# Chunked delta-rule attention with a Mish layer: T~ of 64 tokens merged on TensorE, W = T~K had ahead, attention in fixed bundles

## The chip, the core and the metric

One core of a Trainium2 chip runs the kernel; the time is device time in microseconds from the start of the program to its end. The engines named below work side by side, each through its own list of instructions in order: PE (TensorE, matrix products), DVE (VectorE), ACT (ScalarE), POOL (GpSimd), and SP (SyncE), which issues the loads and stores. Results of TensorE land in PSUM, everything else lies in SBUF, whose 128 rows are the partitions.

## The reference

Four batches of eight heads, 768 tokens, 48 dimensions a head. Each head keeps a state of 48 x 48 that is read and corrected token by token; the outputs of all heads of a token make a row of 384, and go through a layer of width 2048 with Mish.

```python
k_n = k / (norm(k) + 1e-6)
for t in range(S):
    y[:, :, t] = einsum('bhd,bhde->bhe', q[:, :, t], state)
    v_old = einsum('bhde,bhd->bhe', state, k_n[:, :, t])
    state = state + beta_t * einsum('bhd,bhe->bhde', k_n[:, :, t], v_t - v_old)
...
x = y.transpose(0, 2, 1, 3).reshape(B * S, H * D)
h = x @ w_in
sp = where(h > 20, h, log1p(exp(minimum(h, 20))))
out = (h * tanh(sp)) @ w_out
```

## The kernel before

The tokens are cut into 12 chunks of 64. Attention of a chunk is done in matrix form: with c the length of a key plus 1e-6, b' = beta / c^2, V' = c V and L the strictly lower part of K K^T, a chunk solves (I + L b') Z = V' - K S, takes Z~ = b' Z, adds K^T Z~ to the state S, and its output is Y = Q S + lower(Q K^T) Z~. The matrix T~ = b' (I + L b')^-1 turns the solve into a product. The 32 heads are 16 pairs; a pair shares instructions.

**Early part, for two chunks at once (`early`).** VectorE transposes K to `kt`, TensorE makes the Gram blocks `pg`, VectorE masks them to `d` and transposes them to `gt`, so that one block of 32 x 32 lies in each partition. After the norms (`ss`, `nb`, the product at L273) a forward substitution of 30 steps, each one product (`pr`, L290) and one addition (`gt`, L295), gives the inverse; L297 multiplies by b', and L301 transposes to `tt`. For the first group blocks are 16 wide and `merge` completes them. For the second group the steps j = 1 to 17 run on GpSimd and the rest on VectorE; for later groups all run on VectorE.

**Attention of a chunk (`step`), a quarter of the pairs (one batch) at a time.** T~ is had for blocks of 32 tokens only, so a chunk is solved in two halves. `s1`: transpose of Q, Q's and the state's product with K in one go (`gq`, 112 columns), V' less K S. `s2`: Z~ of tokens 0 to 31 (`za`). `s3`: what those do to tokens 32 to 63 (`pr`, L413). `s4`: Z~ of the latter (`zb`). `s5`: Y (`py`, L431) and the new state (`ps`, L437). A tile `xx` for each batch holds, in 64 rows for tokens, Z~, lower(Q K^T) and K and, in the other 64 rows, S, Q^T and rows of the identity. One product with all 128 rows therefore gives Y, and one gives the new state, the identity carrying the old one over.

**The layer (`moe`).** For each chunk there are eight units. `g1`: 18 products to `h`. Then a chain over `e` on ScalarE and VectorE (L509 to L514), a split to `g` (L522, L525). `g2`: 12 products to `acc`. Two tiles of `h` exist, so the third `g1` waits until the first `e` is done. Products are in float32r with values split in a high and a low part. When a chunk's eight units are through, ScalarE copies `acc` to `o` (L551) and the rows are stored.

**The weights** come as float64, in 28 parts (`ri`, `ro`), and are converted on the chip: four instructions of VectorE for most parts (L180, L182, L187, L189 on `mi`, `mo`), two of ScalarE, one of GpSimd (L199).

**The order.** Every piece of work is put on a plan with a time in units of a chunk's layer (`put`); the pieces are written out in the order of these times, a scheduler orders each engine's list for the first part of the plan, and VectorE's instructions that pass `queue` keep their order. Pieces of attention of the next chunk are spread between the units of the layer.

Of the kernel before, what the change touches and what calls it, by code (L numbers as in the profile page):

```python
# [8 lines left out]
F32 = mybir.dt.float32  # L9
# [7 lines left out]
# float32 values whose bits are 0x38000000 and 0x47EFFFFF: the high words of float64s of  # L17
# float32's least and largest exponent
# [15 lines left out]
def kernel(  # L34
# [22 lines left out]
    nc = tc.nc  # L57

    TN = dict(c=[(-2.89,0),(-2.88,0),(-2.8,0),(-2,3),(-1.951,3+3),(-1,11),(0.5,28)],a1=-0.05,a2=0.15,s2a=0.85,s2b=1.1,kp=0,kl=0.15,pp=[0,0.1,0.3,0.5,0.6,0.8],ke=0.1,d0=["k0","k1",1,"b"],d1=["q","v",2,"x",3,"k2",0,"k3",6],p1=-1.4,lo=150,sg=4,wm=14,wpg=8,e1a=-0.7,e1b=0.4,jt=5,wt=46,qk=99,qg=1,qs=1,k2a=-0.95,k2b=-0.6,wmg=18,wz=[4,4,4,4],wgq=2,ma=-0.98,mb=-0.98+0.1,pg=3,fg=1,ps=(1,),e2=1.1,mt=(-1.95,-1.95+0.05),qt=[(-1.95,-1.95+0.1),(-1.6,-1.6+0.1)],st=[(-1.9,-1.9+0.05),(-1.75,-1.75+0.05),(-1.55,-1.55+0.05),(-1.2,-1.2+0.2)],j0=0,j1=18)
# [11 lines left out]
    PB = NP // B  # L71
# [5 lines left out]
    kk = k.rearrange("b (p hh) t d -> hh t (b p) d", hh=2)  # L77
    qq = q.rearrange("b (p hh) t d -> hh t (b p) d", hh=2)
    vv = v.rearrange("b (p hh) t d -> hh t (b p) d", hh=2)
    bt = beta.rearrange("b (p hh) (g t2 c i) -> hh c t2 (b p) g i", hh=2, t2=2, c=2, i=32)  # L80
# [20 lines left out]
    # lmask[p, f] = f >= p % 32 ; amask[(hh,c,j), i] = i > 32c + j  # L101
# [11 lines left out]
    # per batch and head, tokens' rows: Z~ | Aqk^T | K  # L113
    # and rows of d:                    S  | Q^T   | rows of the identity
    W = C + 2 * D
    xx = [cp.tile([P, PB, 2, W], F32, name=f"xx{i}") for i in range(B)]
    for t in xx:
        nc.gpsimd.memset(t[:, :, :, 0:D], 0.0)
        for hh in range(2):
            r = slice(64 - 64 * hh, 128 - 64 * hh)  # L120
            nc.vector.tensor_copy(t[r, :, hh, D + C:], bcast_mid(ident[r, r.start:r.start + D], PB))

    # parts of the weights, each first as float64 and then, in the same place, as high and low parts
# [5 lines left out]
    def load(dst, src):  # L129
        """Loads of the start are issued in this order."""  # L130
        m = nc.sync.dma_start(out=dst, in_=src)  # L131
        if loaded and len(loaded) < TN.get('lo', 150):
            order(m, loaded[-1])
        loaded.append(m)

    def load_src(dst, src, n):
        for hh in range(2):
            for ch in range(2):
                w = 32 if ch == 0 else D - 32
                for tb in range(2):  # L140
                    t0 = C * n + 32 * tb
                    r0 = 64 * (1 - hh) + 32 * ch
                    load(dst[r0:r0 + 32, :, tb, :w], src[hh, t0:t0 + 32, :, 32 * ch:32 * ch + w])

# [13 lines left out]
    def queue(ins, on=True):  # L158
        """VectorE issues what passes here in this order, and the rest where it fits."""
# [11 lines left out]
    def convert(kind, i):  # L171
# [5 lines left out]
        # magnitudes outside float32's exponents go to 0 or the largest  # L177
        # and 2^-80 of the rest has bits that, moved up by 3, are float32's of -|w|
# [5 lines left out]
        # the sign comes by VectorE or, while VectorE is what holds the start up, by the others  # L184
# [18 lines left out]
    kts, tts, nes, ats, vts, dts, tus, yms = {}, {}, {}, {}, {}, {}, {}, {}  # L203

    def early(g):
        dt = ap.tile([P, 2, NP, 32], F32, tag="d", name=f"d{g}", bufs=2)
        split = g < FG
        dts[g] = dt
        for t2 in range(2):
# [5 lines left out]
            kt = kts[n] = ap.tile([P, NP, 2, 32], F32, tag="kt", name=f"kt{n}", bufs=4)  # L215
# [8 lines left out]
            at = ats[n] = ap.tile([P, NP, 32], F32, tag="at", name=f"at{n}", bufs=4)  # L224
            for h8 in range(2):
                ps = pa.tile([P, 8, C], F32, tag="at", name=f"pg{n}_{h8}")
                for p8 in range(8):
                    p = 8 * h8 + p8
                    # rows c = 0: K0 K0^T, K0 K1^T; rows c = 1: K1 K1^T twice
                    for c in range(2):  # L230
                        for hh in range(2):
                            r = slice(64 - 64 * hh, 128 - 64 * hh)
                            r0 = 64 * hh + 32 * c
                            mv = kt[r, p] if c == 0 else kt[r, p, 1:2, :].broadcast_to([64, 2, 32])
# [4 lines left out]
                nc.vector.tensor_tensor(out=dt[:, t2, pr, :], in0=ps[:, :, 0:32],  # L239
                                        in1=bcast_mid(lmask, 8), op=ALU.mult)  # L240
                nc.scalar.copy(out=at[:, pr, :], in_=ps[:, :, 32:])
# [25 lines left out]
        # N[i, j] = -G[i, j] b'_j ; X = (I - N)^-1 in place  # L267
# [32 lines left out]
        tt = tts[g] = ap.tile([P, 2, NP, 32], F32, tag="tt", name=f"tt{g}")  # L300
        queue(nc.vector.transpose(tt.rearrange("p a b i -> p i (a b)"), gt), qg)  # L301
        if split:
# [4 lines left out]
            nc.gpsimd.memset(ym[:, :32, 16:], 0.0)  # L307
        yield

    def merge(n):  # L310
        """T~'s rows 16.. and columns ..15 of each block of 32: -T~22 G21 T~11."""
        g, t2 = n // 2, n % 2
        dt, tt, tu, ym = dts[g], tts[g], tus[g], yms[g][:, NP * t2:NP * t2 + NP]
        pm = {}
# [12 lines left out]
        for h8 in range(2):  # L327
# [6 lines left out]
            if g == 0:  # L334
                keep_warm(TN.get('wmg', 1), m)
            queue(nc.vector.tensor_tensor(out=tt[:, t2, pr, 16:32], in0=tt[:, t2, pr, 16:32], in1=ps, op=ALU.add),
                  n < QS)
            yield

# [5 lines left out]
    def load_v(n):  # L345
        for h8 in range(2):
            vt = vts[n, h8] = ap.tile([P, 8, D], F32, tag="vt", name=f"vt{n}_{h8}", bufs=3)
# [3 lines left out]
    def load_k(n, b):  # L351
        for hh in range(2):
            load(xx[b][64 * hh:64 * hh + 64, :, hh, D + C:], kk[hh, C * n:C * n + C, PB * b:PB * b + PB])

    def step(n, y):
        g, t2 = n // 2, n % 2
        kt, at, ne = kts[n], ats[n], nes[g]

        def scale_v(b):
            vt = vts[n, b // 2][:, PB * (b % 2):PB * (b % 2) + PB, :]  # L360
            nc.gpsimd.tensor_tensor(out=vt, in0=vt,  # L361
                                    in1=bcast_in(ne[:, 16 * t2 + PB * b:16 * t2 + PB * b + PB], D), op=ALU.mult)

        def s1(b, half=None):
            pr = slice(PB * b, PB * b + PB)
            p8 = slice(PB * (b % 2), PB * (b % 2) + PB)
            vt, x = vts[n, b // 2], xx[b]
            if n:
                scale_v(b)
            for hh in range(2 if half != 1 else 0):  # L370
                r = slice(64 - 64 * hh, 128 - 64 * hh)
                queue(nc.vector.transpose(x[r, :, hh, D:D + C], qsrc[r, pr].rearrange("p a b c -> p a (b c)")), n == 0)  # L372
            if half == 0:
                return
            # S is 0 in the first chunk
            d = D if n else 0
            ps = pa.tile([P, PB, C + d], F32, tag="at", name=f"gq{n}_{b}")
            for p in range(PB):
                for hh in range(2):
                    r = slice(64 - 64 * hh, 128 - 64 * hh)  # L380
                    m = nc.tensor.matmul(ps[64 * hh:64 * hh + 64, p, :], kt[r, PB * b + p], x[r, p, hh, D - d:D + C],  # L381
                                         start=True, stop=True)
            if n == 0:
                keep_warm(TN.get('wgq', 1), m)
            if n:
                nc.vector.tensor_tensor(out=vt[:, p8, :], in0=vt[:, p8, :], in1=ps[:, :, 0:D], op=ALU.subtract)
            for hh in range(2):
# [351 lines left out]
```

## Time and profile before

| | |
|---|---|
| time, median of 3 runs (lowest to highest) | 741.7 us (740.0 to 743.1) |
| span of the profiled execution | 745.6 us |
| instructions in it | 22768 |
| TensorE busy, share of the span | 92% |
| VectorE, ScalarE, GpSimd busy | 72%, 63%, 17% |
| granted clock of TensorE, mean | 0.95 |
| weights converted until | 172.7 us |
| first and last output copies | 175.2 us, 734.3 us |

The busy shares are means over stages of unlike kind: the first 200 us have the loads and conversions of the weights, the first chunks' attention and the first units of the layer, the rest is a steady alternation of attention and layer. A row of the chain of waits gives the start, the length and the instructions of one engine on the path that ended last; a row of the grouped view gives a line, its engine and operation, the tile written and the tile read, shapes and count, then the busy time, the mean of one in ns, and the idle time ahead of them. For products in float32 the trace shows two records for each instruction.

### The profile page before, as it was taken

What the parts mean: (1) busy time and instruction counts of PE and PEld (TensorE: products, weight loads), DVE (VectorE), ACT (ScalarE), POOL (GpSimd) and SP (SyncE); (2) the same over time, 40 slices, a digit from 0 to 9 for tenths busy, and PEclk for the clock granted to TensorE, in tenths of its full rate; (3) what the DMA queues carried; (4) which work ended last, traced back from release to release, by engine and by line L of the source; (5) the groups of instructions that cost most, each with busy time, mean ns of one, the idle gap of its engine ahead of it and who ended that gap; (6) DMA issues with size and microseconds to landing.
All of it is one profiled execution on the core that took longest, in us unless ns stands there. A gap on an engine that the chain in (4) does not pass through costs nothing.

```text
span 745.6 us, 22768 instructions
## 1 busy us (share of the span) xinstructions
PE 682.3 (92%) x9656; PEld 602.3 (81%) x9674; DVE 534.3 (72%) x1152; ACT 468.9 (63%) x1005; POOL 127.4 (17%) x171
## 2 busy tenths in 40 slices
PE   5659699878799989999999999999999999999993
PEld 3236588768788878998898998998988989989993
DVE  5796999997747997659995579975499964454351
ACT  2233667755485666776776767767767767767681
POOL 3431336894221221000000000000000000000000
PEclk9756999789899999999999999999999999999998
DMA  5762910253213032122222221130130120000000
GB/s 87 185 181 40 380 32 7 30 84 60 25 32 59 8 54 48 21 44 50 37 34 41 40 38 34 24 51 15 24 59 14 33 49 18 18 23 1 17 7 21
DMA packets 160981, 37.75 MB, mean 51 GB/s; under 512 B 154224, under 2 KB 157296, under 8 KB 160880
## 3 DMA queue, kind: packets, MB, share of 16 engines
q1 hardware_dynamic: 160880, 36.30, 24.0%
q8 instruction: 76, 1.25, 0.7%
q14 instruction: 25, 0.20, 0.1%
HBM read 31.56 MB, written 4.72 MB: 49 GB/s over the span
## 4 chain that ended last, share of the span: by engine, by line
PE 67%; DVE 20%; SPq 4%; issue 3%; ACT 2%; DMA 2%; POOL 1%; DVEq 0%; POOLq 0%; ACTq 0%
PE h L505 24%; PE acc L535 22%; PE gq L381 4%; SPq L131 3%; PE py L431 3%; PE pg L235 2%; PE za L398 2%; DVE pr L290 2%; PE zb L398 2%; PE pr L413 2%; DVE gt L295 2%; PE warm L570 2%; PE ps L437 2%; DVE e L514 1%; DVE xx L389 1%
## 5 line engine op out<-in xcount | busy, mean ns | idle before, releaser
L505 PE MATMUL h<-x,wi 128*128 128x256 f32 x1728 | 238.3, 291 | 13.5 <-DVE e L514 12.1
L505 PEld LDWEIGHTS h<-x,wi 128*128 128x128 f32 x1728 | 218.4, 192 | 23.8 <-DVE e L514 12.5
L535 PE MATMUL acc<-wo,g 128*128 128x384 f32 x1152 | 233.4, 350 | 2.3 <-ACT g L522 1.9
L535 PEld LDWEIGHTS acc<-wo,g 128*128 128x128 f32 x1152 | 201.1, 192 | 8.8 <-ACT g L522 2.5
L514 DVE SCALAR_TENSOR_TENSOR e<-e,h 128x512 f32<-128x512 f32 x96 | 65.8, 685 | 45.5 <-ACT e L513 43.9
L522 ACT CAST g<-e 128x512 fp32r<-128x512 f32 x96 | 59.3, 618 | 49.6 <-DVE e L514 48.6
L361 POOL TENSOR_TENSOR vt<-vt,ne 128x192 f32<-128x192 f32 x48 | 27.3, 589 | 351.9 <-DMA vt<-in_v_dram 187.1
L509 ACT ACTIVATE e<-h 128x512 f32<-128x512 f32 x96 | 57.2, 596 | 47.9 <-PE h L505 45.2
L511 ACT ACTIVATE e<-e 128x512 f32<-128x512 f32 x96 | 60.5, 631 | 33.0 <-DVE e L510 32.5
L510 DVE TENSOR_SCALAR e<-e 128x512 f32<-128x512 f32 x96 | 42.7, 446 | 32.2 <-ACT e L509 31.0
L525 DVE TENSOR_TENSOR g<-e,g 128x512 fp32r<-128x512 f32 x72 | 49.1, 681 | 19.2 <-ACT g L522 18.6
L512 ACT ACTIVATE e<-e 128x512 f32<-128x512 f32 x96 | 60.5, 632 | 2.7
L513 ACT ACTIVATE e<-e 128x512 f32<-128x512 f32 x96 | 60.4, 631 | 2.4
L419 DVE TENSOR_TENSOR vt<-vt,pr 32x192 f32<-32x192 f32 x96 | 34.0, 354 | 32.7 <-PE pr L413 30.9
L290 DVE TENSOR_TENSOR pr<-gt 128x228 f32<-128x228 f32 (+14 forms) x147 | 53.9, 367 | 3.6 <-PE warm L292 0.5
L295 DVE TENSOR_TENSOR gt<-gt,pr 128x228 f32<-128x228 f32 (+14 forms) x147 | 51.5, 350 | 3.3
L372 DVE STREAM_TRANSPOSE xx<-qsrc 64x256 f32<-64x256 f32 x96 | 41.6, 437 | 13.9 <-PE ps L437 9.3
L381 PE MATMUL gq<-xx,kt 64*64 64x112 f32 (+1 forms) x768 | 47.6, 265 | 1.0 <-DVE x L484 1.0
L431 PEld LDWEIGHTS py<-xx 128*64 128x64 f32 x768 | 38.5, 138 | 10.7 <-issue 4.9
L431 PE MATMUL py<-xx 128*64 128x48 f32 x768 | 45.7, 227 | 1.0 <-ACT xx L403 0.3
L525 POOL TENSOR_TENSOR g<-e,g 128x512 fp32r<-128x512 f32 x24 | 31.9, 1328 | 74.1 <-ACT g L522 47.3
L381 PEld LDWEIGHTS gq<-xx,kt 64*64 64x64 f32 x768 | 37.4, 138 | 8.4 <-issue 4.5
(94 smaller groups left out, 838.3 us busy)
## 6 DMA issues: line engine op xcount, KB each, us to landing
ri<-in_moe_w_in_dram SPq DMA_DIRECT2D x12, 512.0 KB
ro<-in_moe_w_out_dram SPq DMA_DIRECT2D x16, 384.0 KB
vt<-in_v_dram SPq DMA_DIRECT2D x48, 96.0 KB
xx<-in_k_dram SPq DMA_DIRECT2D x96, 48.0 KB
out_dram<-o SPq DMA_DIRECT2D x24, 192.0 KB
qsrc<-in_q_dram SPq DMA_DIRECT2D x48, 64.0 KB
ksrc<-in_k_dram SPq DMA_DIRECT2D x44, 64.0 KB
qsrc<-in_q_dram SPq DMA_DIRECT2D x48, 32.0 KB
```

Of the source, the lines that this page charges most:

```text
L290: queue(eng.tensor_tensor(out=pv, in0=nj, in1=xj, op=ALU.mult), on)
L295: queue(eng.tensor_tensor(out=below, in0=below, in1=pv, op=ALU.add), on)
L381: m = nc.tensor.matmul(ps[64 * hh:64 * hh + 64, p, :], kt[r, PB * b + p], x[r, p, hh, D - d:D + C], start=True, stop=True)
L431: nc.tensor.matmul(py[64 * hh:64 * hh + 64, p, :], x[:, p, hh, D:D + C], x[:, p, hh, 0:D], start=True, stop=True)
L505: nc.tensor.matmul(h[:, f2, :], wt["i", f * P // WI * NCH + c][:, i2, f0:f0 + P], x[:, c, :], start=(i == 0), stop=(i == 3 * NCH - 1))
L511: nc.scalar.activation(e, e, AF.Square)
L512: nc.scalar.activation(e, e, AF.Ln, bias=0.5, scale=0.5)
L513: nc.scalar.activation(e, e, AF.Exp, scale=-1.0)
L514: nc.vector.scalar_tensor_tensor(e, e, -1.0, h, op0=ALU.add, op1=ALU.mult)
L522: nc.scalar.copy(out=gg[:, 0], in_=e)
L525: eng.tensor_tensor(out=gg[:, 1], in0=e, in1=gg[:, 0], op=ALU.subtract)
L535: nc.tensor.matmul(acc[t], gg[:, a, f2, ts_], wt["o", f][:, i2, :], start=(f == 0 and i == 0), stop=(f == NF - 1 and i == 2))
```

## The change

- **Pairs.** A pair was two neighbouring heads of one batch. Now it is the same head of batches b and b + 2, and each has 64 rows of its own in all tiles, for tokens and for dimensions alike. Work goes by halves of the pairs (eight) instead of quarters.
- **T~ of 64 tokens.** The two diagonal blocks of 32 come as before. The block off the diagonal is now made by TensorE: `s_a` multiplies the Gram block with T~ of the later half, ScalarE copies it negated; `s_b` multiplies the earlier half's T~ (transposed, `tn`) with that, ScalarE copies it into `tt2`. GpSimd moves the diagonal blocks of the earlier half to their place.
- **W.** `s_w` makes W = T~K once T~ is there, before the state is known; ScalarE copies it negated (`wn`). Then Z~ = T~V' - W S is two products that accumulate in PSUM (`s_z`), one copy. The half-chunk steps `za`, `pr`, `zb` and the subtraction of K S are gone.
- **Y and the state.** Y is two accumulated products (`s_y`), and the state lies in SBUF (`st`) where VectorE adds the product K^T Z~. K comes by loads to `kx`, two tiles a chunk, two chunks deep; the `xx` tiles are gone.
- **Buffers.** Tiles of V go from three to four, those of `kt` from four to three, those of `at` from four to three, `tn` has one.
- **The plan.** The units of the layer have times of their own and run on across chunks. Attention comes in bundles at fixed times: A, B, Q's Gram, W, Z and Y, most with both halves and, for A and B, both chunks of a group.

```diff
-    kk = k.rearrange("b (p hh) t d -> hh t (b p) d", hh=2)
+    kk = k.rearrange("(hh b) h t d -> hh t (b h) d", hh=2)
...
-        tt = tts[g] = ap.tile([P, 2, NP, 32], F32, tag="tt", name=f"tt{g}")
-        queue(nc.vector.transpose(tt.rearrange("p a b i -> p i (a b)"), gt), qg)
+        queue(nc.vector.transpose(tt2[:, :, :, 32:].rearrange("p a b i -> p i (a b)"), gt), qg)
+        tn = tns[g] = ap.tile([P, 2, NP, 32], F32, tag="tn", name=f"tn{g}", bufs=1)
...
+            queue(nc.vector.transpose(tn.rearrange("p a b j -> p j (a b)"), gt.rearrange("p i j -> p j i")), qg)
+            for t2 in range(2):
+                move_diagonal(t2)
...
+        def s_a(h):
+            ps = pa.tile([P, NP, 32], F32, tag="at", name=f"ta{n}")
+            for p in range(NP):
+                for hh in range(2):
+                    r = slice(64 * hh + 32, 64 * hh + 64)
+                    m = nc.tensor.matmul(ps[64 * hh:64 * hh + 32, p, :], at[r, p, :], tt[r, p, 32:], start=True, stop=True)
...
+                nc.scalar.mul(out=at[r], in_=ps[r], mul=-1.0)
+        def s_b(h):
...
+                    m = nc.tensor.matmul(ps[r, p, :], tns[g][r, t2, p, :], at[r, p, :], start=True, stop=True)
...
+                nc.scalar.copy(out=tt[r, :, 32:], in_=ps[r])
+        def s_gq(h):
+            if n:
+                scale_v(h)
+                turn_q(h)
...
+                    m = nc.tensor.matmul(ps[r, p, :], kt[r, PB * h + p], qt[h][r, p, :], start=True, stop=True)
...
+            queue(nc.vector.tensor_tensor(out=aq[h], in0=ps, in1=bcast_mid(amask, PB), op=ALU.mult), n < QS)
+        def s_w(h):
...
+                    m = nc.tensor.matmul(ps[r, p, :], kw(h, p, hh), tt[r, PB * h + p, :], start=True, stop=True)
...
+            nc.scalar.mul(out=wn[h], in_=ps, mul=-1.0)
+        def s_z(h):
...
+                    m = nc.tensor.matmul(pz[r, p, :], tt[r, PB * h + p, :], vts[n, h][r, p, :], start=True, stop=n == 0)
...
+                    m = nc.tensor.matmul(pz[r, p, :], wn[h][d, p, :], st[h][d, p, :], start=False, stop=True)
...
+            nc.scalar.copy(out=vts[n, h], in_=pz)
+        def s_y(h):
...
+                    m = nc.tensor.matmul(py[r, p, :], aq[h][r, p, :], vts[n, h][r, p, :], start=True, stop=n == 0)
...
+                    m = nc.tensor.matmul(py[r, p, :], qt[h][d, p, :], st[h][d, p, :], start=False, stop=True)
...
+                        m = nc.tensor.matmul(ps[r, p, :], kw(h, p, hh), vts[n, h][r, p, :], start=True, stop=True)
...
+                    nc.vector.tensor_tensor(out=st[h], in0=st[h], in1=ps, op=ALU.add)
...
+    for g in range(1, NS // 2):
+        n = 2 * g
+        t0 = n - 2
+        u = TN['c2'] if g == 1 else (0.44, 0.69, 0.87)
+        at(t0 + u[0], (n, A, 0), (n + 1, A, 0), (n, GQ, 0), (n, GQ, 1))
+        at(t0 + u[1], (n, B2, 0), (n + 1, B2, 0))
+        at(t0 + u[2], (n, WW, 0), (n, WW, 1))
+        at(t0 + 1.02, (n, Z, 0), (n, Z, 1))
+        at(t0 + 1.25, (n, Y, 0), (n, Y, 1))
+        at(t0 + 1.5, (n + 1, GQ, 0), (n + 1, GQ, 1))
+        at(t0 + 1.75, (n + 1, WW, 0), (n + 1, WW, 1))
+        at(t0 + 2.02, (n + 1, Z, 0), (n + 1, Z, 1))
+        at(t0 + 2.25, (n + 1, Y, 0), (n + 1, Y, 1))
```

**VectorE around the first unit of the layer.** Before, in the kernel's first part, with conversions of `mi` and `mo` (weights), `e_0` and `e_1` (first units of the layer) and `d`, `gt` (Gram blocks of the second group):

```order
L187 SCALAR_TENSOR_TENSOR mi_1378<-ri_959,mi_1378 128x512
L510 TENSOR_SCALAR e_0_1655<-e_0_1655 128x512
L189 SCALAR_TENSOR_TENSOR mi_1378<-ri_959,mi_1378 128x512
L180 TENSOR_SCALAR mi_1481<-mi_1481 128x512
L239 TENSOR_TENSOR d_1206<-pg_0_1383,lmask 128x256
L182 TENSOR_SCALAR mi_1481<-mi_1481 128x512
L187 SCALAR_TENSOR_TENSOR mi_1481<-ri_961,mi_1481 128x512
L239 TENSOR_TENSOR d_1206<-pg_1_1418,lmask 128x256
L189 SCALAR_TENSOR_TENSOR mi_1481<-ri_961,mi_1481 128x512
L514 SCALAR_TENSOR_TENSOR e_0_1655<-e_0_1655,h_0_1636 128x512
L246 STREAM_TRANSPOSE gt_1454<-d_1206 128x1024
L180 TENSOR_SCALAR mi_1499<-mi_1499 128x512
```

Of the change, where `mo_2087` is the last of the 28 parts, and `gt_1444` with `pr_18`, `pr_19` is the second group's substitution:

```order
L274 TENSOR_TENSOR gt_1444<-gt_1444,nb_1460 128x1024
L279 TENSOR_SCALAR bp_1465<-nb_1460 128x32
L188 SCALAR_TENSOR_TENSOR mo_2087<-ro_938,mo_2087 128x384
L190 SCALAR_TENSOR_TENSOR mo_2087<-ro_938,mo_2087 128x384
L509 TENSOR_SCALAR e_0_1711<-e_0_1711 128x512
L513 SCALAR_TENSOR_TENSOR e_0_1711<-e_0_1711,h_0_1692 128x512
L509 TENSOR_SCALAR e_1_1846<-e_1_1846 128x512
L291 TENSOR_TENSOR pr_18_1673<-gt_1444 128x234
L296 TENSOR_TENSOR gt_1444<-gt_1444,pr_18_1673 128x13x18
L291 TENSOR_TENSOR pr_19_1681<-gt_1444 128x228
L296 TENSOR_TENSOR gt_1444<-gt_1444,pr_19_1681 128x12x19
L513 SCALAR_TENSOR_TENSOR e_1_1846<-e_1_1846,h_1_1827 128x512
```

The end of `e_0` stood among the conversions and stands now behind the last of them; the substitution's 18th step stands ahead of the end of `e_1`.

**GpSimd in the second group's substitution.** Before, its last steps (`pr`, `gt`), with weights (`wo`), `g` of the first layer's units and scalings of V (`vt`) in between:

```order
L290 TENSOR_TENSOR pr_14_1563<-gt_1454 128x238
L295 TENSOR_TENSOR gt_1454<-gt_1454,pr_14_1563 128x17x14
L199 TENSOR_TENSOR wo_1913<-mo_1838,wo_1913 128x384
L290 TENSOR_TENSOR pr_15_1570<-gt_1454 128x240
L295 TENSOR_TENSOR gt_1454<-gt_1454,pr_15_1570 128x16x15
L290 TENSOR_TENSOR pr_16_1574<-gt_1454 128x240
L525 TENSOR_TENSOR g_6_2147<-e_6_2140,g_6_2147 128x512
L295 TENSOR_TENSOR gt_1454<-gt_1454,pr_16_1574 128x15x16
L525 TENSOR_TENSOR g_7_2234<-e_7_2227,g_7_2234 128x512
```

Of the change, from step 10 to 12, and the end of the steps:

```order
L291 TENSOR_TENSOR pr_10_1622<-gt_1444 128x210
L296 TENSOR_TENSOR gt_1444<-gt_1444,pr_10_1622 128x21x10
L526 TENSOR_TENSOR g_0_1718<-e_0_1711,g_0_1718 128x512
L291 TENSOR_TENSOR pr_11_1626<-gt_1444 128x220
L296 TENSOR_TENSOR gt_1444<-gt_1444,pr_11_1626 128x20x11
L291 TENSOR_TENSOR pr_12_1636<-gt_1444 128x228
```

The steps stood beside units 6 and 7 of the first layer; they stand now beside unit 0, and `g_1` comes behind the 17th step.

**TensorE in the first layer and in the steady part.** Before, between units of the layer, in the middle of a chunk, where `zb`, `pr` and `za` are attention of different batches and `acc` and `h` the layer:

```order
L398 MATMUL zb_0_4975<-vt_0_4609,tt_3914 32x48 x2
L535 MATMUL acc_4_4806<-wo_576,g_0_4834 128x384 x2
L535 MATMUL acc_4_4807<-wo_576,g_0_4834 128x384 x2
L398 MATMUL zb_0_4975<-vt_0_4609,tt_3914 32x48 x6
L413 MATMUL pr_1_5018<-xx_99,at_2996 32x48 x4
L535 MATMUL acc_4_4806<-wo_576,g_0_4834 128x384
L535 MATMUL acc_4_4806<-wo_624,g_0_4834 128x384 x3
L535 MATMUL acc_4_4807<-wo_576,g_0_4834 128x384
L535 MATMUL acc_4_4807<-wo_624,g_0_4834 128x384 x3
L413 MATMUL pr_1_5018<-xx_99,at_2996 32x48 x4
L398 MATMUL za_2_5034<-vt_1_4612,tt_3914 32x48 x5
```

Of the change, in the first chunk's layer behind its fifth unit, where `ta` is A of chunks 2 and 3 and `gq` is Q's Gram of chunk 2; it reads `tt_98`, the tile of T~:

```order
L504 MATMUL h_4_2108<-x_0_1035,wi_1558 128x256
L396 MATMUL ta_2137<-tt_98,at_1224 32x32 x32
L396 MATMUL ta_2172<-tt_98,at_1372 32x32 x32
L421 MATMUL gq_0_2210<-qt_0_2208,kt_1137 64x64 x16
L421 MATMUL gq_1_2232<-qt_1_2230,kt_1137 64x64 x16
L538 MATMUL acc_0_2027<-wo_1032,g_2_1905 128x384 x3
L538 MATMUL acc_0_2027<-wo_1133,g_2_1905 128x384 x3
L538 MATMUL acc_0_2028<-wo_1032,g_2_1905 128x384 x3
L538 MATMUL acc_0_2028<-wo_1133,g_2_1905 128x384 x3
L504 MATMUL h_5_2271<-x_0_1035,wi_1452 128x256
```

Small pieces of attention stood between and inside the units of the layer; a bundle holds one kind of product of all pairs, and the bundle of A stands behind the fifth `h` of chunk 0 in TensorE's list.

More of the change, by code (lines that the diff above doesn't have):

```diff
@@ L355, in step, with steps @@
-    def step(n, y):
+            dst = kx[2 * (n % 2) + h][64 * hh:64 * hh + 64, :PB * D].rearrange("r (p d) -> r p d", d=D)
+            load(dst, kk[hh, C * n:C * n + C, PB * h:PB * h + PB])
+    def steps(n):
         g, t2 = n // 2, n % 2
[L357 to L378, printed above, removed]
-                for hh in range(2):
[L380 to L387, printed above, removed]
-                r = slice(64 * hh, 64 * hh + 64)
-                queue(nc.vector.tensor_tensor(out=x[r, :, hh, D:D + C], in0=ps[r, :, d:],
-                                              in1=bcast_mid(amask[r], PB), op=ALU.mult), n < QS)
-        def solve(b, c):
-            pz = pa.tile([P, PB, D], F32, tag="at", name=f"z{"ab"[c]}{n}_{b}")
-            for p in range(PB):
-                for hh in range(2):
-                    r = slice(64 * hh + 32 * c, 64 * hh + 32 * c + 32)
-                    m = nc.tensor.matmul(pz[r, p, :], tts[g][r, t2, PB * b + p, :],
-                                         vts[n, b // 2][r, PB * (b % 2) + p, :], start=True, stop=True)
@@ L529, in g2 @@
             gg = gs.pop(fp)
+            if fp == 0:
+                acc.extend(po.tile([P, DM], F32, tag=f"acc{t}", name=f"acc{t}_{n}") for t in range(NTT))
             for t in range(NTT):
@@ L642, with at, run, warmed @@
     put(one(loads, TN.get('d1', ["q", "v", 2, "k2", 2, "k3", 2, "x", 22])), 1, -2.901, -2.901)
-    put(attend0, 1, -2.3, -2.3)
+    chunk = {}
+    def at(t, *work):
+        def run():
+            for n, i, h in work:
+                if n < NS:
+                    if n not in chunk:
+                        chunk[n] = steps(n)
+                    chunk[n][i](h)
+            yield
+        put(run(), 1, t, t)
+    def warmed(t, n, i, h):
+        def run():
+            chunk[n][i](h)
+            keep_warm(8, last[-1])
+            yield
+        put(run(), 1, t, t)
+    at(-2.3, (0, SCALE, 0), (0, SCALE, 1))
     put(one(loads, TN.get('d2', [28])), 1, TN.get('p1', -1.2) + 0.001, TN.get('p1', -1.2) + 0.001)
@@ new lines @@
+    todo1 = [(n, fp) for n in range(NS) for fp in range(NFP)]
+    todo2 = list(todo1)
+    t = 0.0
+    lag = 2
+    for k, (n, fp) in enumerate(todo1):
+        t = n + (fp + 0.25) / NFP
+        put(one(units[n][0], fp), 1, t, t)
+        if n == NS - 1 and fp == 2:
+            lag = 3
+        elif k >= lag:
+            m, fq = todo2.pop(0)
+            t = n + (fp + 0.75) / NFP
+            put(one(units[m][1], fq), 1, t, t)
+    for i, (m, fq) in enumerate(todo2):
+        put(one(units[m][1], fq), 1, NS + i, NS + i)
@@ new lines @@
+    for n in range(1, NS):
+        t = n - 0.5 / NFP
+        put(one(turn, n), 1, t, t)
+        t = TN['p1'] if n == 1 else TN['p2'] if n == 2 else n - 1.9
+        put(one(prep, n), 1, t, t)
+        if n > 1:
+            t = max(0.6, n - 2.4)
+            put(one(lambda n=n: [load_k(n, h) for h in range(2)]), 1, t, t)
+    put(merge(1), 4, TN['ma'], TN['mb'])
+    t1 = TN['c1']
+    at(t1[0], (1, A, 0), (1, GQ, 0))
+    at(t1[1], (1, B2, 0), (1, GQ, 1))
+    at(t1[2], (1, WW, 0), (1, WW, 1))
```

269 lines of the change are left out of this document (119 added, 150 removed).

## The prediction

> **What bounds the kernel now.** I read the page's busy times and the shares of its chain first, then busy time by stretch, then the chain itself in the steady part and at the end, and last the start.
>
> ```profile
> PE 682.3 (92%) x9656; PEld 602.3 (81%) x9674; DVE 534.3 (72%) x1152; ACT 468.9 (63%) x1005; POOL 127.4 (17%) x171
> PE 67%; DVE 20%; SPq 4%; issue 3%; ACT 2%; DMA 2%; POOL 1%; DVEq 0%; POOLq 0%; ACTq 0%
> ```
>
> TensorE is busy 92% of the span and holds two thirds of the chain that ended last; VectorE holds a fifth. The stretches tell where (columns: from:to and length; busy time of PE, PEld, DVE, ACT, POOL; granted clock, DMA share, GB/s).
>
> ```profile
> 80.00:120.00 40.00, 32.41 (x785) 26.91 (x789) 39.07 (x76) 25.29 (x57) 14.58 (x13) 0.96 0.42 149
> 120.00:150.00 30.00, 27.18 (x316) 24.03 (x312) 28.11 (x41) 21.11 (x47) 24.38 (x31) 0.83 0.16 24
> 150.00:178.00 28.00, 22.39 (x193) 21.02 (x190) 27.44 (x52) 16.10 (x34) 22.74 (x28) 0.88 0.54 75
> 178.00:200.00 22.00, 15.81 (x91) 15.17 (x90) 14.20 (x30) 9.29 (x16) 3.86 (x3) 0.84 0.28 46
> 440.00:492.00 52.00, 51.83 (x642) 47.00 (x642) 48.59 (x127) 36.03 (x78) 3.33 (x7) 1.00 0.18 33
> 492.00:545.00 53.00, 53.00 (x880) 48.26 (x881) 30.91 (x62) 37.61 (x82) 1.26 (x3) 1.00 0.17 32
> ```
>
> There are two regimes. Up to about 178 us VectorE is full (39.07 of 40, 28.11 of 30, 27.44 of 28): it converts the weights. From then on TensorE is full, 105 us for two chunks (440 to 545). So the change has to be priced twice: what it does to VectorE's work before about 175 us, and to TensorE's work afterwards.
>
> **The steady part.** The chain gives TensorE's prices (start, length, what, number of records).
>
> ```profile
> 450.28 0.91 PE gq L381 x16
> 466.20 2.33 PE h L505 x18
> 469.50 2.31 PE acc L535 x12
> 477.55 0.25 PE py L431 x4
> 477.81 0.09 PE ps L437 x4
> 477.89 0.12 PE py L431 x4
> 478.43 0.09 PE ps L437 x4
> 494.13 0.33 PE xt L481 x3
> ...
> 711.13 2.08 PE acc L535 x12
> 713.22 2.14 PE h L505 x18
> ...
> L551 ACT ACTIVATE o<-acc x24: 485/493/494, 175.2 to 734.3; 128x384 f32<-128x384 f32 x24
> ```
>
> At the end, without attention, a unit of the layer takes 2.14 + 2.08 = 4.22 us, so two chunks of eight units 67.5. With attention in between an h takes 2.33 and an acc 2.31, about 0.2 more, and the first py of a bundle 0.25 where the next has 0.12: an interruption costs about 0.33 us by itself.
>
> A pair of heads is four records (two heads, two passes). py loads 64 columns of weights and moves 48: from 477.81 to 478.43 there are three rounds of ps and py, 0.207 each, less 0.09 for ps, so 0.118 a pair. ps loads 48 and moves 48: 0.09. gq loads 64 and moves 112: 0.91 / 4 = 0.23.
>
> ```profile
> 202.05 0.46 PE za L398 x16
> 202.51 1.03 PE pg L235 x64
> ```
>
> None of the new products stands in this trace in its form: all are 64 rows by 64 columns of weights moving 48 or 64 columns, in two quarters of the array. The nearest row is py's, 0.118; below it ps has 0.09, and pg, with four small tiles at once, 1.03 / 16 = 0.064; above it gq has 0.23 for nearly double the columns. I take 0.118 and keep 0.09 for the range. Per chunk, 16 pairs: Z has two products, T~V' and W S, 32 x 0.118 = 3.78; Y has two, 3.78; S, Q's Gram and W one each, 1.89. A and B, of 32 rows and columns, lie between za's 0.46 / 4 = 0.115 a pair for 48 columns and pg's 0.064: I take pg's, 1.05 each, since only 32 columns move; za's would add 1.6 a chunk. The turn of Y costs 0.7. That is 16.0 a chunk, 32.1 for two, with the Gram blocks (four times 1.03, 4.1) 36.2.
>
> The order has nine bundles in two chunks (and the two turns). They cost 9 x 0.33 = 3.0, and 0.8 for the two turns and the changes of product inside bundles. So two chunks take 67.5 + 36.2 + 3.8 = **107.5 us against 105**: the fewer interruptions are outweighed by the separate products of W, Z and Y, which before came in one product with 128 rows or rode along in gq's 112 columns. Over the five pairs of chunks 2 to 11 this is +12.5.
>
> **The start.** Before, VectorE takes e_0 between conversions, at 103.9, and ends the last conversion at 172.7.
>
> ```profile
> L514 DVE SCALAR_TENSOR_TENSOR e<-e,h x4: 673/687/687, 103.9 to 124.8; 128x512 f32<-128x512 f32 x4
> ...
> 172.19 0.55 DVE L189 SCALAR_TENSOR_TENSOR mo<-ro,mo 128x384 int32<-128x384 int32 x1
> ```
>
> Now every conversion stands ahead of e_0 on VectorE (first pair of fences in the section on the change). Between 43.5 and 172.8 these go or fall behind the last conversion:
>
> ```profile
> L389 DVE TENSOR_TENSOR xx<-gq,amask 64x256 f32<-64x256 f32 x24 | 10.1, 419 | 1.2 <-PE gq L381 1.0
> L372 DVE STREAM_TRANSPOSE xx<-qsrc 64x256 f32<-64x256 f32 x24 | 10.0, 431 | 0.9 <-PE py L431 0.4
> L419 DVE TENSOR_TENSOR vt<-vt,pr 32x192 f32<-32x192 f32 x16 | 5.7, 354 | 5.9 <-PE pr L413 5.4
> L514 DVE SCALAR_TENSOR_TENSOR e<-e,h 128x512 f32<-128x512 f32 x8 | 5.5, 686 | 0.2
> L510 DVE TENSOR_SCALAR e<-e 128x512 f32<-128x512 f32 x9 | 5.3, 601 | 0.0
> L386 DVE TENSOR_TENSOR vt<-vt,gq 128x192 f32<-128x192 f32 x8 | 2.8, 348 | 0.1
> ...
> L304 DVE STREAM_TRANSPOSE tu<-gt 128x512 f32<-128x512 f32 x1 | 1.0, 1003 | 0.0
> ```
>
> 39.4 us go. Six transposes of 128x512 (L304's 1.0 each), four masks of that size (at L514's 0.69) and two copies of state (at most 0.69) come: about 10.1. The conversions then end at 172.7 - 29.3 = 143.4, or 5.9 earlier if the wait for pr goes too; I take **138**, since pr itself is gone.
>
> But h_2 waits for e_0, and VectorE's solve of the second group's T~ (pr_18 on), ahead of e_1's end, waits for GpSimd's 17 steps, which begin only after the gt x nb product, three rows ahead of the last conversion, at 136.5. In before this solve lay beside conversions.
>
> ```profile
> L295 POOL TENSOR_TENSOR gt<-gt,pr 128x238 f32<-128x238 f32 (+14 forms) x17 | 11.2, 659 | 0.8
> L290 POOL TENSOR_TENSOR pr<-gt 128x238 f32<-128x238 f32 (+14 forms) x17 | 11.2, 658 | 0.6
> L525 POOL TENSOR_TENSOR g<-e,g 128x512 fp32r<-128x512 f32 x6 | 8.4, 1404 | 2.4 <-ACT g L522 2.4
> L199 POOL TENSOR_TENSOR wo<-mo,wo 128x384 fp32r<-128x384 f32 x7 | 7.4, 1053 | 3.3 <-ACT wo L198 3.0 <-PE zb L398 0.3
> ...
> L290 DVE TENSOR_TENSOR pr<-gt 128x228 f32<-128x228 f32 (+14 forms) x147 | 53.9, 367 | 3.6 <-PE warm L292 0.5
> L295 DVE TENSOR_TENSOR gt<-gt,pr 128x228 f32<-128x228 f32 (+14 forms) x147 | 51.5, 350 | 3.3
> ...
> L525 DVE TENSOR_TENSOR g<-e,g 128x512 fp32r<-128x512 f32 x56 | 38.0, 678 | 11.0 <-ACT g L522 10.8
> L301 DVE STREAM_TRANSPOSE tt<-gt 128x1024 f32<-128x1024 f32 x4 | 8.2, 2053 | 0.0
> L297 DVE TENSOR_TENSOR gt<-gt,bp 128x1024 f32<-128x1024 f32 x4 | 4.9, 1224 | 0.3
> ```
>
> GpSimd: 22.4 for 34 operations, 1.05 for a wo and 1.40 for g_0 in between, so 161.4. VectorE: 26 operations of 0.36 (9.3), e_1's and e_2's three (1.8), two transposes and two additions (3.2), the product with bp (1.2) and the transpose to T~ (2.1): **179.0**. There TensorE waits at A of chunk 2, which the order places behind h_4 (third pair of fences). From there it has 96 units of 4.22 less five h and two acc (14.9), 390.2; attention of chunks 2 to 11, ten times 16.0, four times 4.1 for Gram blocks, chunk 1's turn, less the last S, 175.5; interruptions five times 3.8, 18.9: 584.6 in all. Then 11.3 from the last output copies' start to the end (745.6 less 734.3, the row of L551). 179.0 + 584.6 + 11.3 = 774.9 against the profiled span of 745.6: +29.3, of which 12.5 is the steady part and 17 the start. That span is 3.9 above the median of the runs, 741.7; I put the difference on the median: **771 us**.
>
> **Edits put at nothing.** Loads of K that came late before (waits between 150 and 200) are now early, but T~ is later still, so nothing is gained by them. ScalarE, at 36 to 38 us of 52 in the steady rows, loses four half-row copies of Z~ a batch and gets the copies of A, B, W and Z whole; TensorE's own work covers them, as A and B stand a unit or two of the layer apart and W and Z more. If that cover were gone, an A to B wait would be a copy of 0.5 us, five times. VectorE's additions to the state (two a chunk, at most 0.69 each) lie behind Y, and the next reader, Z, comes three quarters of a chunk later. GpSimd moves diagonal blocks in stretches where it has 1 to 3 us of work in 52.
>
> **Rivals.** First, the opposite side: the bundles let products overlap more than py's row shows. The price decides: 112 products of pairs a chunk over ten chunks make 1 ns 1.12 us, so below 0.092 the kernel is no slower and below 0.088 it is faster by over 0.5%; at 0.080 it takes some 728, at pg's 0.064 711. If only the 80 that move 48 columns came at ps's 0.09, it would take 749. For it speaks pg; against it that pg has four tiles at once and these have two, as py and gq. By the row of ps against py, the same moved columns cost 0.09 with 48 columns of weights and 0.118 with 64, so weights are paid for. The Trainium skill says in "TensorE: Matmul & The Clock Gate" (Step-by-step: what each phase is for) that the next tile's weights load while this tile's matmul runs, and that a load's time scales with its columns. By the first half a product would cost what its moved columns cost, 0.09 at most for the 80, so 749 or less; the 28 ns between py and ps, for the same moved columns, agree with the second half.
>
> Second, the start isn't waited for: T~ is ready before TensorE needs it. TensorE would then run from 138 with 584.6, the 10.6 of layer ahead of A from h_2 on, and 12.3 of chunk 1's W, Z and Y: 138 + 607.5 + 11.3 = 757, so 753. The order speaks against it.
>
> Third, VectorE becomes the bound in each group's solve: from the Gram blocks to T~ it has 60 steps (21.5), transposes and products (8.2) and ten or so pieces of the layer (10), 40 us, while TensorE has 45 between them. Of five us of slack, little is left if e waits too. Five us late in each of four groups gives 791. The row of 440 to 492 (48.59 of 52) shows that VectorE is nearly full there already.
>
> The clock is a small risk: the rows up to 200 show 0.83 to 0.88 where TensorE waits. By the page named (Part 1: The HAM clock gate) activity of about 3.4 us releases the throttle; that would add under 2 us behind the wait, an estimate.
>
> **How the numbers follow.** The forecast, start late and products at py's price, has 0.52 (755 to 787). The 749 and the early T~ have 0.22 together: 0.13 for one alone or a part of each (746 to 755), 0.09 for a mixture that ends within 738 to 745. Products below 0.092 a pair have 0.17, of which 0.15 end under 738 and 0.02 within. A late solve has 0.09 (about 791). The range reaches from 739 to 789: it leaves out the 0.15 below and about half of the late solves. A measurement of this kernel can tell about 0.5% from no change, 738 to 745. Faster 0.15, same 0.11, slower 0.74.
>
> **What would show it.** In the profile after: conversions' last row near 138; VectorE's pr_18 waiting for GpSimd for some 20 us; TensorE waiting for the transpose to tt until near 179; the first output copy some 25 to 30 us later than now (175.2 to near 205); a Z of 3.8, W of 1.9 and 107 to 108 us from copy to copy over two chunks. Wrong would be a Z under 3, or T~ ready before 165.

## The result

The changed kernel takes 784.3 us (median of 4 runs, 781.2 to 786.5) against 741.5 us before (740.0 to 743.1): a ratio of 1.058, 95% interval 1.054 to 1.062, 42.9 us more. Its profiled execution spans 780.7 us. The forecast was 771 us, with a range of 739 to 789. Two runs that took far longer than all others of their kernel, 1227.2 us of the kernel before and 914.6 of the last variant in experiment 6, are left out of the figures below.

The page's first part and the shares of the chain, of the change:

```profile
PE 696.1 (89%) x11761; PEld 653.4 (84%) x11778; DVE 460.4 (59%) x889; ACT 412.9 (53%) x747; POOL 136.7 (18%) x173
...
PE 61%; DVE 24%; issue 3%; SPq 3%; ACT 3%; POOL 3%; DMA 1%; DVEq 0%; ACTq 0%; POOLq 0%
```

VectorE has 74 us less to do than before, and yet holds more of the chain; TensorE has 14 us more. Busy time by stretch, of the change (columns as in the prediction):

```profile
80.00:120.00 40.00, 25.08 (x658) 18.77 (x660) 37.51 (x60) 17.13 (x33) 15.57 (x14) 0.54 0.27 55
120.00:150.00 30.00, 23.07 (x448) 21.81 (x448) 14.45 (x29) 12.67 (x25) 22.39 (x36) 0.86 0.13 21
...
131.00:154.00 23.00, 16.34 (x362) 15.59 (x357) 3.48 (x6) 7.76 (x14) 20.48 (x37) 0.96 0.24 36
...
150.00:178.00 28.00, 15.47 (x228) 15.24 (x230) 20.57 (x40) 8.08 (x15) 9.77 (x13) 0.66 0.07 9
178.00:200.00 22.00, 22.00 (x340) 21.14 (x338) 6.63 (x10) 16.40 (x29) 4.47 (x4) 0.97 0.10 13
...
440.00:492.00 52.00, 52.00 (x864) 50.66 (x862) 42.64 (x103) 26.38 (x49) 2.87 (x3) 1.00 0.23 40
492.00:545.00 53.00, 52.15 (x976) 50.57 (x972) 26.83 (x42) 34.11 (x62) 4.09 (x6) 1.00 0.23 39
```

Both regimes are still there. Up to about 130 us VectorE is full (37.51 of 40), then it has little to do for 23 us (3.48 of 23) while GpSimd is full (20.48 of 23), and from 178 on TensorE is full. What happens in between stands in the chain of the change:

```profile
131.24 0.40 POOL pr L291
...
153.56 0.66 POOL gt L296
154.24 0.41 DVE pr L291
...
169.66 1.92 DVE tt L303
171.71 3.62 PE ta L396 x128
175.34 3.61 PE gq L421 x64
```

GpSimd's 17 steps run from 131.2 to 154.2, VectorE's rest from there to the transpose at 169.7, and A (`ta`) starts at 171.7: every step of the forecast's start, each some five to seven us earlier. The last conversion and the ends of the first units, from VectorE's rows of `mo` and of `e` (least, median and longest duration, then first and last start):

```profile
L190 DVE SCALAR_TENSOR_TENSOR mo<-ro,mo x16: 557/558/1500, 43.2 to 131.6; 128x384 int32<-128x384 int32 x16
...
L513 DVE SCALAR_TENSOR_TENSOR e<-e,h x3: 678/680/691, 136.7 to 161.0; 128x512 f32<-128x512 f32 x3
```

The last conversion ends at 132.2 (131.6 and 0.56 for its last instruction). e_0 ends its chain behind it, at 136.7, where before it stood at 103.9; the last of these three, e_2, comes at 161.0, behind GpSimd. The steady part, in the chain of the change, from one A bundle to the next:

```profile
283.27 2.17 PE ta L396 x128
...
394.77 2.14 PE ta L396 x128
396.92 2.01 PE gq L421 x64
...
416.34 2.01 PE pw L430 x64
...
439.97 0.93 PE ps L463 x32
...
501.38 2.14 PE ta L396 x128
...
610.93 2.14 PE ta L396 x128
```

From 394.77 to 501.38 two chunks take 106.6 us, a stretch in which TensorE doesn't wait at all; the two before it take 111.6 and 111.5, the one behind it 109.6. An A of both chunks is 2.14, W and Q's Gram 2.01 each, the state's product 0.93 for half of the pairs.

What TensorE waits for behind the first A of the second group (chunks 2 and 3), of the change (total, times, longest):

```profile
PE h L504 <- DVE e L513: 4.9, 3, 3.7
PE acc L538 <- POOL g L526: 2.6, 1, 2.6
PE pg L236 <- issue: 1.4, 2, 0.8
PE h L504 <- DVE x L482: 0.6, 1, 0.6
```

**The profile of before, taken again.** It spanned 745.6 us where the runs' median is 741.5. One run profiled the same kernel once more.

> The kernel before, unchanged, profiled once more, since the profile of before (745.6) is 6 us above what its runs say (741.5 less some 1.7 around the span). If the difference lies in the start, e_0 comes at 96 to 98 and the last conversion near 163 (as in b3 and b4, whose edits come later), and everything behind the first output copy keeps its distances. If it lies in the steady part, two chunks there take under 104 us instead of 105.

It took 741.1 us, with a span of 739.6. Rows of 40 to 80 us, first of the profile of before, then of the second one, and VectorE's row of `e` in the second:

```profile
40.00:80.00 40.00, 32.87 (x673) 22.41 (x683) 30.85 (x60) 15.96 (x43) 11.90 (x14) 0.62 0.52 140
...
40.00:80.00 40.00, 30.50 (x836) 21.23 (x852) 37.17 (x71) 20.07 (x55) 13.56 (x14) 0.87 0.72 211
...
L514 DVE SCALAR_TENSOR_TENSOR e<-e,h x4: 675/688/689, 98.0 to 119.0; 128x512 f32<-128x512 f32 x4
```

The transfers ran at 140 GB/s in the one and 211 in the other, VectorE was busy 6 us longer, and e_0 came at 98.0 instead of 103.9. The first output copy stands at 169.4 instead of 175.2, and from there to the last both take 559 us. The profile on which the prediction was made had a start some 6 us longer than the second one. Against 739.6 the change's span is 41.1 us longer, close to the 42.9 of the medians.

### The profile page after: what moved, and what is told of

Same layout as the page of the kernel before. It is cut to its first block, busy times and chain, and to the rows that moved or that the text cites. A ratio compares the mean times of both kernels' runs of the same rounds, so it can differ in the third digit from the quotient of the medians.

```text
span 780.7 us, 26324 instructions
## 1 busy us (share of the span) xinstructions
PE 696.1 (89%) x11761; PEld 653.4 (84%) x11778; DVE 460.4 (59%) x889; ACT 412.9 (53%) x747; POOL 136.7 (18%) x173
## 4 chain that ended last, share of the span: by engine, by line
PE 61%; DVE 24%; issue 3%; SPq 3%; ACT 3%; POOL 3%; DMA 1%; DVEq 0%; ACTq 0%; POOLq 0%
PE h L504 20%; PE acc L538 20%; DVE pr L291 4%; DVE gt L296 4%; SPq L132 3%; PE gq L421 3%; PE pg L236 2%; PE pz L439 2%; PE pw L430 2%; PE py L454 2%; PE ta L396 2%; PE pz L442 2%; PE py L457 2%; DVE e L513 2%; PE tb L408 2%
## 5 line engine op out<-in xcount | busy, mean ns | idle before, releaser
L504 PE MATMUL h<-x,wi 128*128 128x256 f32 x1728 | 230.2, 288 | 14.3 <-DVE e L513 13.7
L538 PE MATMUL acc<-wo,g 128*128 128x384 f32 x1152 | 221.9, 342 | 2.6 <-POOL g L526 2.6
L382 POOL TENSOR_TENSOR vt<-vt,ne 128x384 f32<-128x384 f32 x24 | 24.9, 1044 | 217.4 <-DVE nb L266 143.1
L296 DVE TENSOR_TENSOR gt<-gt,pr 128x228 f32<-128x228 f32 (+14 forms) x147 | 49.1, 334 | 4.0
L439 PE MATMUL pz<-vt,tt 64*64 64x48 f32 x768 | 45.4, 222 | 1.2 <-issue 1.2
L454 PE MATMUL py<-vt,aq 64*64 64x48 f32 x768 | 44.8, 219 | 0.0
L442 PE MATMUL pz<-st,wn 48*64 48x48 f32 x704 | 41.7, 218 | 0.5 <-ACT wn L433 0.5
L457 PE MATMUL py<-st,qt 48*64 48x48 f32 x704 | 42.1, 218 | 0.0
L439 PEld LDWEIGHTS pz<-vt,tt 64*64 64x64 f32 x768 | 38.2, 137 | 4.2 <-issue 3.1
L454 PEld LDWEIGHTS py<-vt,aq 64*64 64x64 f32 x768 | 37.1, 134 | 3.5 <-issue 3.4
```

Source lines behind the costliest of these rows:

```text
L296: queue(eng.tensor_tensor(out=below, in0=below, in1=pv, op=ALU.add), on)
L439: m = nc.tensor.matmul(pz[r, p, :], tt[r, PB * h + p, :], vts[n, h][r, p, :], start=True, stop=n == 0)
L454: m = nc.tensor.matmul(py[r, p, :], aq[h][r, p, :], vts[n, h][r, p, :], start=True, stop=n == 0)
L504: nc.tensor.matmul(h[:, f2, :], wt["i", f * P // WI * NCH + c][:, i2, f0:f0 + P], x[:, c, :], start=(i == 0), stop=(i == 3 * NCH - 1))
L538: nc.tensor.matmul(acc[t], gg[:, a, f2, ts_], wt["o", f][:, i2, :], start=(f == 0 and i == 0), stop=(f == NF - 1 and i == 2))
```

## The experiments

**1. Where the second group's steps run.** One number of the table:

```diff
-ps=(1,)
+ps=()
```

> All 30 steps of the second group's substitution run on VectorE; GpSimd does none (nothing is left out). Theory A, the start: the first A bundle waits for this T~, and T~ waits for GpSimd's 17 steps (23 us from 131.2 to 154.2). On VectorE they take 34 x 0.36 = 12 us, so A starts at about 161 instead of 171.7, and the whole time falls with it, by 9 to 12 us, to 772 to 775. Rival B: the start is set by the conversions and the first units e_0 to e_2, which on VectorE now wait behind more steps; A starts between 168 and 175 and the time stays within 3 us of the change's 784.

772.95 us (771.2 to 775.8), a ratio of 1.040 to before: 11.4 us less than the change. TensorE's waits from 130 to 178, first of the change, then of this kernel:

```profile
PE h L504 <- DVE e L513: 8.8, 1, 8.8
PE ta L396 <- DVE tt L303: 5.9, 1, 5.9
...
PE h L504 <- DVE e L513: 5.8, 2, 3.4
```

A no longer waits for T~, and the wait for e is 3 us shorter. In the chain of this kernel, A starts 8.1 us earlier than in the change:

```profile
163.63 2.21 PE ta L396 x127
```

A and Q's Gram then take 4.8 us instead of 7.2. Theory A holds: GpSimd's steps, which in the kernel before lay beside conversions, are on the path that sets the end.

**2. Without the products with the state.** The second product of Z and of Y is left out, in `s_z` and `s_y` alike:

```diff
-start=True, stop=n == 0)
-for r in heads if n else ():
+start=True, stop=True)
+for r in ():
```

> Leaves out the second product of Z (W S) and of Y (Q S) in chunks 1 to 11, 32 pairs a chunk. If TensorE alone bounds the steady part and a pair costs py's 0.118 us, 32 x 0.118 x 11 = 41.5 us go, to 743; at 0.09 a pair 32 us, to 752. Rival: VectorE's substitution for the next group is full behind TensorE, so that what goes between the second Gram bundle and A (one Z and one Y of each of four groups, 15 us) turns into waiting of TensorE; then 24 to 28 us go, to 756 to 760, and the A bundle waits 3 to 6 us more in each group.

745.3 us (740.9 to 748.5): 39 us less by the medians. The two profiled executions are 33.9 us apart; this kernel's was the slowest of its ten runs. In the trace a Z of both halves went from 3.87 to 2.00 us and a Y of one half from 1.88 to 0.97, taken from the first product of a bundle to the first of the next: 3.7 us a chunk, 41 us over eleven chunks, so 0.116 a pair, close to the 0.118 priced. Most of what went from TensorE went from the time, more than the rival's 24 to 28. The rival was right that something is given back: TensorE's waits behind the first A grew from 9.5 to 16.8 us, and the largest are for `x`, the turned Y on its way into the layer:

```profile
PE h L504 <- DVE x L482: 5.3, 4, 2.1
PE pg L236 <- DVE x L482: 5.2, 1, 5.2
```

From the second A on, two chunks take 102.6, 101.2 and 103.5 where the change takes 111.5, 106.6 and 109.6, so 8.9, 5.4 and 6.1 less for 7.4 us of work. The start isn't the same either: in this kernel's list TensorE has seven h and four acc ahead of the first A, which starts at 176.9 and waits for nothing, where the change has five and two.

**3. Bundles cut in two.** Five lines of the schedule, such as

```diff
-        at(t0 + 1.25, (n, Y, 0), (n, Y, 1))
+        at(t0 + 1.25, (n, Y, 0))
+        at(t0 + 1.31, (n, Y, 1))
```

> Same work; five bundles of each pair of chunks (Z and Y of both chunks, W of the second) are cut in two halves with one h of the layer between. If an interruption costs 0.33 us of TensorE, 5 x 5 x 0.33 = 8 us more, to 790 to 793, less what falls in waits of TensorE for T~ (2 us). Rival, that cutting the layer costs nothing by itself: 784 within 2 us. That would mean that bundling saved nothing.

782.1 us (780.6 to 782.8), ratio 1.052 (1.046 to 1.058): no slower than the change, with 25 more interruptions. Its waits of TensorE behind the first A, to be read against the change's four rows above:

```profile
PE h L504 <- DVE x L482: 1.7, 1, 1.7
PE pg L236 <- issue: 1.6, 3, 0.8
```

They fell from 9.5 to 3.3 us. What the cuts cost the waits give back. The cost can be read where TensorE waits in neither kernel, the third stretch of two chunks from A to A, in this kernel's chain:

```profile
391.71 2.14 PE ta L396 x128
499.72 2.14 PE ta L396 x128
```

It takes 108.0 us here and 106.6 in the change (394.77 to 501.38). Five cuts cost 1.4 us, or 0.28 each, near the 0.33 that the prediction priced. The time is the rival's, 784 within 2, but its reading, that a cut costs nothing, isn't right: the longer bundles save nothing in the end because they come with waits of their own.

**4. 48 columns of weights for the new state.** In `s_y`, with VectorE's additions by heads:

```diff
-ps[r, p, :], kw(h, p, hh), vts
+ps[r.start:r.start + D, p, :], kw(h, p, hh)[:, :D], vts
```

> The new state's product loads 48 columns of weights instead of 64 (VectorE adds each head's 48 rows apart, two more instructions a bundle half; nothing is left out). If loaded columns set the price of a pair (0.118 at 64, 0.09 at 48), ps takes 0.72 instead of 0.93 for eight pairs and 16 x 0.027 x 11 = 4.8 us go, to 779 to 781. Rival, that the 48 moved columns or a fixed price set it: ps stays at 0.93 and the time within 1.5 us of the change's, or a little above for VectorE's extra instructions.

783.8 us (781.1 to 785.3): the 4.8 us expected did not come. In the chain of this kernel `ps` takes 0.72 for half of the pairs where the change has 0.93 (the row at 439.97 above):

```profile
440.70 0.72 PE ps L463 x32
```

The price was as said, 0.090 a pair, though the moved columns are the same; 4.6 us of TensorE went, and the time did not fall by as much. In this trace T~'s transpose starts at 173.6 instead of 169.7 and the last instruction of the conversions at 134.9 instead of 131.6. Whether that is this kernel's or its execution's, one profile doesn't tell.

**5. The layer's first units ahead.** Two attempts at fixed times, alone and with experiment 1.

> Only fixed times of the plan change: chunk 1's bundles come behind the first units of the layer instead of ahead of them, and the first A bundle behind all eight units of chunk 0 instead of five. GpSimd keeps its 17 steps. Theory A2: at the start TensorE lacked work that its list would let it do (it waited 9.1 us for e_1 and 6.2 us for T~ before the first A, both behind GpSimd's steps); with all eight units ahead of A it works through that time and most of the 15.3 us go, to 770 to 775. Rival A: only an earlier T~ helps; T~ is as late as before (171.7), so the time stays within 4 us of 784.

> The edit of e6 and the edit of e1 (all steps on VectorE) together. If both remove the same waits (theory: 15.3 us of TensorE's waiting at the start is all there is to win), it ends where the better of the two does, within 3 us. If each removes something of its own, the gains add: 760 to 764.

They took 788.3 and 786.2 us. These two kernels compute something else in chunk 1: its Z is put behind the transpose that writes the second group's T~ into the one buffer, so it takes that T~ and waits for it, and half of its queries are those of chunk 2, since their load comes ahead in the program. TensorE waits 11.6 us ahead of that Z in the first of them and 3.8 in the second; the question stays open by them. Repeated with the transpose moved behind Z:

```diff
-...,e1c=0.42,...,c1=(-0.8,-0.6,-0.4,0.1,0.3),c2=(0.55,0.7,0.86),...
+...,e1c=0.6,...,c1=(0.05,0.17,0.3,0.42,0.55),c2=(0.8,0.92,1.0),...
```

> The change with other fixed times, e6 made right: chunk 1's bundles behind the first units of the layer, the first A behind seven h instead of five, and the transpose to the second group's T~ behind chunk 1's Z in the program (one buffer for T~). GpSimd keeps its steps, T~ comes at 172 to 176. Theory A2 (TensorE lacked work that its list let it do): two h and three acc, 10.5 us, are done ahead of A that waited behind it, less 2 to 4 for a later A; 774 to 778. Rival A (only an earlier T~ helps): 784 within 3.

> The edits of e8 and of e1 (all steps on VectorE). If both remove the same 15.3 us of waiting at the start, the better of e1 (773) and e8 within 3 us. If they add: 762 to 766. VectorE then has steps between the first units, so e_1 to e_6 come later than in e8.

776.5 us (775.7 to 777.6) and 774.2 us (772.8 to 775.6); half of chunk 1's queries are still chunk 2's, at the same work. So the list of TensorE was worth 7.8 us, and together with experiment 1 no more than experiment 1 alone. That both remove the same waits fits this; it isn't shown beyond the times. The waits of e8 from 90 to 178:

```profile
PE tb L408 <- ACT at L400: 11.1, 1, 11.1
PE ta L396 <- DVE tt L303: 7.6, 1, 7.6
PE pg L236 <- DVE tt L347: 5.2, 2, 4.1
```

Part of the win went into new waits, the longest for ScalarE's copy between A and B of chunk 1. e_0 came at 132.0 even here, behind 26 of the 28 conversions.

**6. The start of the kernel before.** Could the change's later transposes of K help the kernel before? One number of its table (`e2`, 1.1 to 1.6), the same with four tiles of V, and 1.5:

> The kernel before, with the start of the third group's early part moved 0.5 of a chunk's layer later in the plan (nothing else). Its transposes of K stand between VectorE's steps for the second group's T~, where one waits 6.95 us for its load at 188 and three take 3.7 us. The change has these transposes behind T~. If the start of before waits for this T~ (first za of chunk 2 at 202), T~ comes 8 to 10 us earlier and the time falls by as much, to 732 to 735. Rival: units of the layer or GpSimd's steps hold T~ anyway; 741 within 3 us.

> As b3, and four tiles of V instead of three, as the change has them, so that the loads of weights no longer stand behind the second load of V on the queue (until 72 us in the kernel before). If weights held VectorE's conversions (it was idle 9 us between 40 and 80), 3 to 9 us less than b3. Rival: it was idle there for chunk 0's attention; b3 within 2 us.

> The kernel before with the third group's early part 0.4 later instead of b3's 0.5: the first transpose of K stays where it was, the two others go behind the second group's T~. If b3 lost by the third group's T~ being late (302 against 285) what it won by the second's (184 against 198), half of the move keeps the gain at chunk 1 and gives back less: 736 to 741. Rival: every move of this part later is given back and more; 745 to 751.

751.3 (748.4 to 756.5), 750.4 (749.5 to 751.7) and 745.1 us (743.1 to 752.1), ratios of 1.014 (1.008 to 1.020), 1.011 (1.007 to 1.016) and 1.006 (1.001 to 1.011): none is faster than before, and all lie a little above it, the last one barely beyond the scatter. VectorE's transposes to T~ in the first 305 us, of before (second profile), b3 and b5; first and last of three:

```profile
L301 DVE STREAM_TRANSPOSE tt<-gt x3: 1948/1972/2094, 40.3 to 279.6; 128x1024 f32<-128x1024 f32 x3
...
L301 DVE STREAM_TRANSPOSE tt<-gt x3: 1952/2072/2096, 38.8 to 302.5; 128x1024 f32<-128x1024 f32 x3
...
L301 DVE STREAM_TRANSPOSE tt<-gt x3: 1941/2026/2095, 39.3 to 292.8; 128x1024 f32<-128x1024 f32 x3
```

The second group's T~ came at 184 and 183 instead of 193, but the third's at 302.5 and 292.8 instead of 279.6, which goes with more given back than won. The fourth tile of V made no difference. No version was found that beats both kernels.

## Why the prediction came out

**The steady part was right.** 107.5 was forecast for two chunks, 106.6 is the undisturbed figure, against 105 before; Z 3.87 (3.78 forecast), W and Q's Gram 2.01 (1.89), A 1.07 a chunk (1.05). These prices are measured in the change's own trace, 0.121 a pair for Z, and experiment 2 shows that nearly all of such work is paid for in time: the first rival, cheaper products, falls. The switches cost 0.28 us each by experiment 3 (0.33 forecast). So the interruptions saved are indeed outweighed by the products of W, Z and Y.

**The start was right in its mechanism, and T~ 7.3 us early.** Conversions ended at 132.2 (138 forecast), GpSimd took 23.0 us (24.9), VectorE 17.5 to A (17.6). Experiment 1 shows that this chain is on the path. The second rival, that T~ isn't waited for, falls with it; experiment 1 and the runs e8 and e9 say that without this wait some 8 to 11 us go, not the 18 that this rival's 753 implied. What keeps the start long then is that the layer has no unit done before about 130: e_0 at 136.7 against 98.0, the conversions all ahead of it. That this is the rest of the loss is argued from the rows, not shown; a kernel that takes e_0 among the conversions wasn't tried. One sign of the prediction did not come: the first output copy stands at 212.9, not near 205, though A was earlier. In the change's trace Z of chunk 2, Gram blocks of the third group and two h of the next chunk's layer run ahead of it, so it doesn't mark the end of the start as it did before.

**What failed in the sum: the waits behind A, put at nothing.** From A to the end 595.9 were forecast and 609.0 taken. Waits of TensorE behind A, for which the sum has no term, are 9.5: 4.9 for e, 2.6 for g behind a load of V on GpSimd, 2.0 others. The third rival named this (VectorE nearly full in each solve), with five us late in each of four groups; the waits of the four stretches from A to A are 4.3, 2.8, none and 2.3. The clock cost more than the two us that the prediction named as a risk: A and Q's Gram took 3.62 and 3.61 at 171.7 where they take 2.14 and 2.01 later, 3.1 us, and the granted clock was 0.50 there:

```profile
171.70:179.00 7.30, 7.29 (x193) 7.12 (x193) 3.86 (x5) 4.76 (x9) 3.70 (x5) 0.50 0.02 4
```

The shorter pairs gave back 4.5. That leaves 5 us. About 2.8 of them are products that run slow behind the two longest waits of the 9.5: the h at 275.3 takes 3.77 where 2.30 is usual, and the acc around 294.8 takes 3.62 without its wait where 2.27 is usual, at granted clocks of 0.54 and 0.59. The rest isn't resolved.

**The base.** The difference was made against a profile whose start was 6 us longer than the second one's, and put on the median. So the parts are these: 29.3 forecast, plus 6.0 for the base, less 7.3 for T~, plus 13.1 behind A, make the 41.1 between the change's profile and the second one of before. The forecast's 771 is below the measured 784 by the base and by the waits, two terms that were mis-sized, not by another mechanism; the early T~ hid part of both. That the time lies inside the range is in part luck: with A at 179.0, as forecast, and all else as measured, it would be some 791 us (784.3 + 7.3, an estimate), above the 789 of the range.

## What to carry to other kernels

Price a bundle by what it adds to the bounding engine, not by the switches it saves: here the products of W, Z and Y, 0.12 us a pair and 112 pairs a chunk, weighed more than switches of 0.28 us, and longer bundles brought waits of their own. When work is moved off a full engine at the start, ask what stands behind it in each engine's list: the chain that had lain beside the conversions became the path as soon as they ended early. And take the profile that a sum is made against twice, or check that its span fits the runs.

## What the runs showed of the hardware

Two profiles of one kernel differ by 6 us in the start, with transfers at 140 and 211 GB/s between 40 and 80 us. For pairs of products that move 48 columns, 64 columns of weights cost 0.116 us and 48 cost 0.090; the Trainium skill's sentence that a load's time scales with its columns ("TensorE: Matmul & The Clock Gate", Step-by-step: what each phase is for) agrees, while the overlap that the same section tells of didn't make 64 as cheap as 48. After a wait of 5.9 us TensorE stayed slow for A and Q's Gram, at a granted clock of 0.50 from 171.7 to 179.0: 7.2 us, where the two take 4.15 later. That is twice the 3.4 us of activity with which the prediction reckoned, so the trace doesn't agree with it there; behind the shorter wait of 3.7 us at 275.3 the one slow h took 3.77.
